# Block-causal attention and a rational FFN in float32 on one core: the causal mask moved from a matmul of its own into the unused half of the score passes' operands

## The chip, the cores and the metric

The kernel runs on one core of a Trainium2 chip. The core has a matrix engine (TensorE, PE in the profile, with its weight loads as PEld), a vector engine (VectorE, DVE), a scalar engine for activations and copies (ScalarE, ACT), GpSimd (POOL) and SyncE (SP), which here does nothing but issue transfers to the core's 16 DMA engines. Engines work on SBUF, 128 partitions wide; PE writes its sums into eight banks of PSUM. Each engine runs its instructions in the order that was fixed when the kernel was built, and waits on semaphores.

The metric is the device time of one execution in microseconds.

## The reference

Attention over 8 batches, 8 heads, 576 positions and 64 channels, with a causal mask by blocks of 64 positions, and then an FFN over the 4608 tokens whose activation is a quotient of polynomials; all in float32:

```python
scores = (1.0 / np.sqrt(D)) * np.matmul(q, k.transpose(0, 1, 3, 2))
mask = (pos[:, None] // 64) >= (pos[None, :] // 64)
scores = np.where(mask, scores, -1000000000.0)
scores = scores - np.max(scores, axis=-1, keepdims=True)
attn = np.exp(scores)
attn = attn / (np.sum(attn, axis=-1, keepdims=True) + 1e-09)
x = np.matmul(attn, v)            # then [B*S, H*D] = [4608, 512]

h = x @ w_in                      # [4608, 2048]
P = a[0] + a[1] * h + a[2] * h**2 + a[3] * h**3
Q = 1.0 + abs(b[0]) * abs(h) + abs(b[1]) * h**2
out = (P / (Q + 1e-06)) @ w_out   # [4608, 512]
```

## The kernel before

**Numbers in two parts.** Float32 precision is kept by splitting every operand into a high part h and a low part l that the matrix engine takes in one pass each.

**A pair of heads at a time.** The 32 pairs of heads (8 batches, 4 pairs each) are worked on one after the other. `load` brings q, k and v of a pair. `prep(p, 0)` transposes q of both heads on PE (L355) and writes its high part with ACT (L359) and its low part with DVE (L360) into a tile `hl`; `prep(p, 1)` does the same with k. `hl` has four slots of 576 columns, q high, k high, k low, q low, and one buffer: rows 0 to 63 belong to head 0, rows 64 to 127 to head 1. As soon as k is there too, three transfers for each head (L369 to L371) make a tile `kq` of it, over 128 rows: in the head's own rows q high, k high, k low, and in the other 64 rows q low, k high, k low. There are three buffers of `kq` (KQB), two of them for each pair.

**Scores.** `scores(p, t, j)` works on head j and query tile t (64, 128, 128, 128 and 128 queries against 64, 192, 320, 448 and 576 keys; the fifth in two pieces of 288). The first pass (L421) multiplies [q high; q low] by [k high; k high], the second (L422) by [k low; k low], so that both passes use all 128 rows. For t > 0 a third matmul in bf16 (L425) adds -2^30 where the first 64 queries of the tile meet the last 64 keys: `mrow` has it in row 0 of its first 64 columns, `mcol` has a one there. The row's maximum is taken by DVE (L426). `expo`, one step later, does the exponential on ACT (L438) and the division on DVE and POOL (L444 to L451). `transp` transposes the probabilities on PE (L470), and splits them (L475, L476) into `pt0`, `pt1` and `pt2`; `pv` multiplies them by v, for tiles 0 to 2 together and for tiles 3 and 4 together (L489), splits the result into a tile `xs` (L492, L493), and stores it to a scratch tensor `xscr` in DRAM (L494). Scores, transposes, products with v and the transposes of `prep` share five PSUM banks (`ps_a`); for the first four pairs some of them use the FFN's banks too.

**FFN.** It runs in units of 256 tokens by 256 hidden columns: `first` (24 matmuls, L201), an activation over ACT, POOL and DVE (L208 to L226), a split (L233, L234) and `second` (12 matmuls, L250). The hidden columns are done in two phases, 10 of the 16 blocks of 128 in phase 0, 6 in phase 1. Phase 0 runs between the steps of attention as soon as whole batches are done; phase 1 begins when attention has given its memory back. Weights are split into parts by the kernel itself, early on.

**Order.** `attn_steps` goes through 320 steps (pair, tile, head), ten to a pair. In a pair's steps the next pair is loaded at step 0 and prepared at steps 3 (q) and 5 (k); `transp` follows its scores by nine steps, `pv` by ten. The FFN gets its half-units spread over the steps (UP, UN, HOLD): from step 93 to step 333, 134 of them. This order of the program is a priority, not the order of execution: at build time a scheduler with a model of the engines' times goes through the instructions, issues what can run by then, hands out the buffers of a tag as they come free, and so fixes the queue of each engine.

Of the kernel before, what the change touches and what calls it, by code (L numbers as in the profile page):

```python
# [9 lines left out]
F32 = mybir.dt.float32  # L10
F32R = mybir.dt.float32r
I32 = mybir.dt.int32
U32 = mybir.dt.uint32
BF16 = mybir.dt.bfloat16
AF = mybir.ActivationFunctionType
ALU = mybir.AluOpType
AX = mybir.AxisListType
# [3 lines left out]
B, H, S, D = 8, 8, 576, 64  # L21
# [6 lines left out]
LEND = 4  # L28
RL = 3
C0 = 0  # L30
KQB = 3
XB = 3
HOLD = 6
ALAG3 = 10
# [9 lines left out]
LAG = (1, 2, 3)  # L44
GBUFS = 2
CBUFS = 2
NFA = 10
NFB = NF - NFA
NU = (NFA // 2, NFB // 2)
LP = 96  # L50
NL = S // LP
QSCALE = 0.125
NEG = -float(2 ** 30)
# [6 lines left out]
def attn_ffn_kernel(  # L60
# [11 lines left out]
    nc = tc.nc  # L72
    nc.scalar.preload_act_table_set("natural_log_exp_and_others")

    cpool = ctx.enter_context(tc.tile_pool(name="const", bufs=1))
    dpool = ctx.enter_context(tc.tile_pool(name="scratch", bufs=1, space=DRAM))
    ffn = ctx.enter_context(tc.tile_pool(name="ffn", bufs=2))
# [8 lines left out]

    ident = cpool.tile([128, 128], F32, name="ident")
    make_identity(nc, ident)
    mrow = cpool.tile([128, 128], BF16, name="mrow")
    mcol = cpool.tile([128, 64], BF16, name="mcol")  # L90
    nc.vector.memset(mrow, 0.0)
    nc.vector.memset(mrow[0:1, 0:64], NEG)
    nc.vector.memset(mcol, 0.0)
    nc.vector.memset(mcol[0:1, :], 1.0)
    coef = cpool.tile([128, 6], F32, name="coef")
    nc.gpsimd.dma_start(out=coef[:, 0:4], in_=ca.partition_broadcast(128))
    nc.gpsimd.dma_start(out=coef[:, 4:6], in_=cb.partition_broadcast(128))
# [198 lines left out]
    NK = [64, 192, 320, 448, 576]  # L296

    wpool = ctx.enter_context(tc.tile_pool(name="wA", bufs=1))
    with ExitStack() as actx:
        att = actx.enter_context(tc.tile_pool(name="att", bufs=2))  # L300
        apers = actx.enter_context(tc.tile_pool(name="apers", bufs=1))
# [2 lines left out]
        pt0 = [apers.tile([128, 1, 320], F32R, name=f"pt0{x}") for x in "hl"]  # L304
        pt1 = [apers.tile([128, 4, 256], F32R, name=f"pt1{x}") for x in "hl"]
        pt2 = [apers.tile([128, 9, 256], F32R, name=f"pt2{x}") for x in "hl"]

        vpad = [apers.tile([128, 128 + 4 * 192], F32R, name=f"vp{x}") for x in "hl"]
        for x in pt1:
# [2 lines left out]
            nc.vector.memset(x[:, 7:9, 0:128].bitcast(F32), 0.0)  # L312
        for x in vpad:
            nc.vector.memset(x.bitcast(F32), 0.0)


        NP = B * NPAIR
# [26 lines left out]
        def prep(p, which):  # L344

            s = st_[p]
            if which == 0:
                s["hl"] = att.tile([128, 4, S], F32R, name=f"hl{p}", tag="hl", bufs=1)
            raw, sc = (s["qr"], s["kr"])[which], (QSCALE, 1.0)[which]
            hl = s["hl"]  # L350
            h, l = (hl[:, 0], hl[:, 3]) if which == 0 else (hl[:, 1], hl[:, 2])
            for half in range(2):
                ps = bank(p - 1, f"tp{p}_{which}_{half}")[:, :3 * LP].rearrange("p (c t) -> p c t", c=3)
                for c in range(3):
                    nc.tensor.transpose(ps[:, c, :], raw[:, half * 3 + c].rearrange("p j d -> p (j d)"),  # L355
                                        ident[:LP, :LP])
                cs = slice(half * 288, half * 288 + 288)
                pf = ps.rearrange("p c t -> p (c t)")
                nc.scalar.activation(out=h[:, cs], in_=pf, func=AF.Copy, scale=sc)  # L359
                nc.vector.scalar_tensor_tensor(out=l[:, cs], in0=pf, scalar=sc, in1=h[:, cs].bitcast(F32),  # L360
                                               op0=ALU.mult, op1=ALU.subtract)
            if which == 1:


                for j in range(2):
                    kq = att.tile([128, 3, S], F32R, name=f"kq{p}_{j}", tag="kq", bufs=KQB)
                    src = hl[64 * j:64 * j + 64].bitcast(F32)
                    other = kq[64 - 64 * j:128 - 64 * j].bitcast(F32)
                    nc.sync.dma_start(out=kq[64 * j:64 * j + 64].bitcast(F32), in_=src[:, 0:3])  # L369
                    nc.sync.dma_start(out=other[:, 1:3], in_=src[:, 1:3])  # L370
                    nc.sync.dma_start(out=other[:, 0], in_=src[:, 3])  # L371
                    s["kq", j] = kq

        def vprep(p):
            vr = st_[p]["vr"]
# [24 lines left out]
        def pieces(t):  # L400
            return [(0, NK[t])] if t < 4 else [(0, 288), (288, 288)]

        def scores(p, t, j):
            s = st_[p]
            nq = NQ[t]
            if j == 0:
                pt = att.tile([128, 2, NK[t]], F32, name=f"p{p}_{t}", tag=f"p{t}", bufs=1)

                pk = att.tile([128, 2, 64], F32, name=f"pk{p}_{t}", tag="pk", bufs=2) if t > 0 else pt
                nm = att.tile([128, 2, 2], F32, name=f"nm{p}_{t}", tag="nm", bufs=4)  # L410
                sm = att.tile([128, 2, 2], F32, name=f"sm{p}_{t}", tag="sm", bufs=4)
                s[t] = (pt, pk, nm, sm)
            pt, pk, nm, sm = s[t]
            kq = s["kq", j]
            qs = slice(Q0[t], Q0[t] + 128)
            banks = []
            for i, (c0, w) in enumerate(pieces(t)):
                ww = max(w, 256)
                ps = ps_a.tile([128, 512], F32, name=f"s{p}_{t}_{j}_{i}", tag="a")
                last = t > 0 and c0 + w == NK[t]  # L420
                nc.tensor.matmul(ps[:, :ww], lhsT=kq[:, 0, qs], rhs=kq[:, 1, c0:c0 + ww], start=True, stop=False)  # L421
                nc.tensor.matmul(ps[:, :ww], lhsT=kq[:, 0, qs], rhs=kq[:, 2, c0:c0 + ww],  # L422
                                 start=False, stop=not last)
                if last:
                    nc.tensor.matmul(ps[:, w - 64:w], lhsT=mrow, rhs=mcol, start=False, stop=True)  # L425
                nc.vector.reduce_max(out=nm[:nq, j, i:i + 1], in_=ps[:nq, :w], axis=AX.X, negate=True)  # L426
                banks.append(ps)
            if t == 4:
                nc.vector.tensor_tensor(out=nm[:, j, 0:1], in0=nm[:, j, 0:1], in1=nm[:, j, 1:2], op=ALU.min)
            s[t, j] = banks  # L430
# [24 lines left out]
        def transp(p, t):  # L455
            pt, pk, _, _ = st_[p].pop(t)
            nq = NQ[t]
            nb = 1 + 2 * t
            groups = {1: [1], 3: [1, 2], 5: [1, 4], 7: [4, 3], 9: [3, 3, 3]}[nb]
            blk = 0  # L460
            for gi, gn in enumerate(groups):
                ps = bank(p, f"t{p}_{t}_{gi}").rearrange("p (c t) -> p c t", c=4)
                for i in range(gn):
                    x = blk + i
                    if x == 0:
                        src = pk[:nq].rearrange("q j k -> q (j k)")
                    else:
                        key = 64 + 128 * ((x - 1) // 2)
                        src = pt[:nq, (x - 1) % 2, key:key + 128]
                    nc.tensor.transpose(ps[:, i, :nq], src, ident[:nq, :nq])  # L470
                (hi, lo), b0, c0 = ((pt2, blk, Q0[t] - 320) if t > 2 else (pt0, 0, Q0[t]) if blk == 0 else
                                    (pt1, blk - 1, Q0[t] - 64))
                dh = hi[:, b0:b0 + gn, c0:c0 + nq]
                dl = lo[:, b0:b0 + gn, c0:c0 + nq]
                nc.scalar.copy(out=dh, in_=ps[:, :gn, :nq])  # L475
                nc.vector.tensor_tensor(out=dl, in0=ps[:, :gn, :nq], in1=dh.bitcast(F32), op=ALU.subtract)  # L476
                blk += gn

        def pv(p, g):
            b, hp = divmod(visits[p][0], NPAIR)  # L480
            vh, vl = vpad
            nb, w = ((5, 320), (9, 256))[g]
            o = ps_a.tile([128, 512], F32, name=f"o{p}_{g}", tag="a")
            for x in range(nb):
                s0 = 64 if (g == 0 and x > 0) else 0
                hi, lo = ((y[:, x] for y in pt2) if g else (y[:, 0] for y in pt0) if x == 0 else
                          (y[:, x - 1] for y in pt1))
                for i, (vv, pp) in enumerate(((vh, lo), (vh, hi), (vl, hi))):
                    nc.tensor.matmul(o[:, s0:w], lhsT=vblock(vv, x), rhs=pp,  # L489
                                     start=(x == 0 and i == 0), stop=(x == nb - 1 and i == 2))  # L490
            xs = att.tile([128, 2, 320], F32R, name=f"x{p}_{g}", tag="xs", bufs=1)
            nc.scalar.copy(out=xs[:, 0, :w], in_=o[:, :w])  # L492
            nc.vector.tensor_tensor(out=xs[:, 1, :w], in0=o[:, :w], in1=xs[:, 0, :w].bitcast(F32), op=ALU.subtract)  # L493
            nc.sync.dma_start(out=xscr[b][:, hp, :, g * 320:g * 320 + w], in_=xs[:, :, :w].bitcast(F32))  # L494
# [40 lines left out]

        wts, wsteps = split_weights(wpool, 0, NFA, F32R)
        load(0)
# [82 lines left out]
```

## Time and profile before

| | us |
|---|---|
| median of 3 runs | 1390.15 (1389.13 to 1396.89) |
| the profiled execution | 1389.48 |
| its span, first to last instruction | 1387.7 |
| PE busy | 1294.4 (93%) |
| DVE busy | 1029.0 (74%) |
| POOL busy | 955.3 (69%) |
| ACT busy | 909.7 (66%) |
| score passes, first to last start | 17.1 to 961.1 |
| DMA packets in 40 slices, total | 200.93 MB, mean 145 GB/s |

Busy times are unions of instructions' durations. Matmuls are pipelined: the duration of one is longer than the distance to the next, so what a matmul costs is read from start to start. A row of the timeline gives the start, the time from the first start to the last end, engine, line, operation, tiles, shape, how many in a row, and in brackets how long the engine was idle before and what ended it. A row that ends in `xN` and begins with `SPq` is the issue of a transfer; when it has landed is told by the list of DMA issues, as a median from issue to landing.

### The profile page before, as it was taken

Reading aid. Unit: us, or ns where it says so; the run is one execution under the profiler, and the core shown is the slowest. Engines: PE = TensorE matmul, PEld = TensorE weight load, DVE = VectorE, ACT = ScalarE, POOL = GpSimd, SP = SyncE. Lnnn points to the kernel's source line nnn. Section 1 sums busy time; section 2 is a strip of 40 time slices with the busy share of each in tenths; the row PEclk is TensorE's granted clock in tenths of the full one; section 3 lists DMA queues with packets and bytes.
Section 4 is the critical chain, followed back from the end, with each engine's and each line's share of the span. In section 5 each row is a group of like instructions: output and inputs, shape, how many; then the busy total and the mean of one; then the engine's idle time right before and its main releaser. Section 6 shows DMA issues by size and latency. Waiting matters only on the chain.

```text
span 1387.7 us, 25820 instructions
## 1 busy us (share of the span) xinstructions
PE 1294.4 (93%) x8736; PEld 1165.6 (84%) x8736; DVE 1029.0 (74%) x2048; ACT 909.7 (66%) x2250; POOL 955.3 (69%) x1240
## 2 busy tenths in 40 slices
PE   4677899999899989999999999999989999999998
PEld 3567788989788878888989999999979998999897
DVE  5898877788778867887767777766756676776665
ACT  4676777777677766776767777776545555555553
POOL 4888877687777757777767676766556655565564
PEclk9787899999999999999999999999999999999999
DMA  9778566666656665675654565651711333333332
GB/s 214 199 196 234 146 148 161 158 165 184 149 142 154 162 167 141 156 178 136 164 133 113 150 151 123 152 139 46 259 59 60 107 122 122 122 122 122 122 122 91
DMA packets 225635, 200.93 MB, mean 145 GB/s; under 512 B 132064, under 2 KB 195552, under 8 KB 225504
## 3 DMA queue, kind: packets, MB, share of 16 engines
q1 hardware_dynamic: 225440, 199.28, 54.2%
q8 instruction: 70, 1.15, 0.3%
q14 instruction: 61, 0.50, 0.1%
q0 software_dynamic: 64, 0.00, 0.0%
HBM read 98.57 MB, written 44.04 MB: 103 GB/s over the span
## 4 chain that ended last, share of the span: by engine, by line
PE 72%; DVE 9%; DMA 6%; POOL 5%; ACT 4%; issue 2%; SPq 1%; DVEq 0%; POOLq 0%; ACTq 0%
PE h L201 26%; PE o L250 25%; PE o L489 9%; PE t L470 4%; PE s L421 3%; PE s L422 3%; PE tp L355 2%; DMA x<-xscr 2%; DMA kq<-hl 2%; DVE nm L426 1%; ACT p L438 1%; POOL gl L234 1%; DVE v L225 1%; DVE u L224 1%; DMA xscr<-x 1%
## 5 line engine op out<-in xcount | busy, mean ns | idle before, releaser
L201 PE MATMUL h<-x,wih 128*128 128x256 f32 x2304 | 446.3, 289 | 12.0 <-DMA x<-xscr 7.9
L201 PEld LDWEIGHTS h<-x,wih 128*128 128x128 f32 x2304 | 372.3, 194 | 21.6 <-issue 7.6
L201 PE MATMUL h<-x,wil 128*128 128x256 f32 x1152 | 331.0, 287 | 0.0
L250 PE MATMUL o<-woh,gl 128*128 128x512 f32 x576 | 232.2, 403 | 7.9 <-POOL gl L234 6.8
L210 POOL TENSOR_SCALAR v<-u,bab 128x512 f32<-128x512 f32 x144 | 120.2, 835 | 165.0 <-ACT u L208 162.6
L250 PE MATMUL o<-woh,gh 128*128 128x512 f32 x576 | 227.9, 396 | 0.0
L250 PE MATMUL o<-wol,gh 128*128 128x512 f32 x576 | 227.0, 394 | 0.0
L426 DVE TENSOR_REDUCE nm<-s 128x1 f32<-128x288 f32 (+4 forms) x384 | 161.4, 427 | 84.8 <-PE s L425 49.9
L201 PEld LDWEIGHTS h<-x,wil 128*128 128x128 f32 x1152 | 223.2, 194 | 0.4
L234 POOL TENSOR_TENSOR gl<-s,gh 128x512 fp32r<-128x512 f32 x144 | 188.4, 1309 | 50.2 <-ACT gh L233 47.2
L438 ACT ACTIVATE p<-s,nm 128x288 f32<-128x288 f32 (+4 forms) x384 | 184.6, 484 | 47.1 <-DVE nm L426 34.8
L211 POOL TENSOR_TENSOR u<-v,u 128x512 f32<-128x512 f32 x144 | 190.2, 1321 | 9.8
L451 POOL TENSOR_SCALAR p<-p,rc 128x128 f32<-128x128 f32 (+3 forms) x256 | 165.0, 656 | 31.6 <-DVE rc L446 29.3
L208 ACT ACTIVATE u<-h 128x512 f32<-128x512 f32 x144 | 86.0, 597 | 123.5 <-PE h L201 116.9
L218 ACT ACTIVATE v<-u,qcb 128x512 f32<-128x512 f32 x144 | 104.6, 726 | 92.0 <-POOL u L211 91.4
L421 PE MATMUL s<-kq 128*128 128x256 f32 (+3 forms) x384 | 136.3, 357 | 24.0 <-DMA kq<-hl 11.2
L212 DVE TENSOR_TENSOR s<-s,h 128x512 f32<-128x512 f32 x144 | 98.6, 685 | 69.8 <-ACT s L209 68.9
L250 PEld LDWEIGHTS o<-woh,gl 128*128 128x128 f32 x576 | 109.4, 190 | 28.3 <-POOL gl L234 9.0
L250 PEld LDWEIGHTS o<-wol,gh 128*128 128x128 f32 x576 | 108.7, 189 | 22.4
L250 PEld LDWEIGHTS o<-woh,gh 128*128 128x128 f32 x576 | 109.3, 190 | 16.0
L470 PE MATMUL t<-ident,p 128*128 128x128 f32 (+1 forms) x672 | 113.0, 279 | 7.2 <-POOL p L451 2.3
L422 PE MATMUL s<-kq 128*128 128x256 f32 (+3 forms) x384 | 119.0, 312 | 0.0
(105 smaller groups left out, 2993.6 us busy)
## 6 DMA issues: line engine op xcount, KB each, us to landing
kq<-hl SPq DMA_DIRECT2D x64, 432.0 KB, 4.2
x<-xscr SPq DMA_DIRECT2D x96, 256.0 KB, 3.6
kq<-hl SPq DMA_DIRECT2D x64, 288.0 KB, 5.4
xscr<-x SPq DMA_DIRECT2D x32, 320.0 KB, 4.7
qr<-in_q_dram SPq DMA_DIRECT2D x64, 144.0 KB, 2.8
kr<-in_k_dram SPq DMA_DIRECT2D x64, 144.0 KB, 2.7
kq<-hl SPq DMA_DIRECT2D x64, 144.0 KB, 4.9
pscr<-os SPq DMA_DIRECT2D x18, 512.0 KB, 3.3
```

The source lines that it names most:

```text
L201: nc.tensor.matmul(h[:, j, :], lhsT=w[:, dc, fs], rhs=xs[dc // 2][:, dc % 2, hl, :], start=(dc == 0 and i == 0), stop=(dc == 3 and i == 2))
L210: nc.gpsimd.tensor_scalar(out=vt, in0=ut, scalar1=b1, scalar2=b0, op0=ALU.mult, op1=ALU.add)
L211: nc.gpsimd.tensor_tensor(out=ut, in0=vt, in1=ut, op=ALU.mult)
L234: nc.gpsimd.tensor_tensor(out=gl.rearrange("p j t -> p (j t)"), in0=st, in1=gh.rearrange("p j t -> p (j t)").bitcast(F32), op=ALU.subtract)
L250: nc.tensor.matmul(self.o[m], lhsT=g[:, j, ms], rhs=w[:, f, :], start=(u == 0 and j == 0 and i == 0), stop=(u == nu - 1 and j == 1 and i = ...
L421: nc.tensor.matmul(ps[:, :ww], lhsT=kq[:, 0, qs], rhs=kq[:, 1, c0:c0 + ww], start=True, stop=False)
L422: nc.tensor.matmul(ps[:, :ww], lhsT=kq[:, 0, qs], rhs=kq[:, 2, c0:c0 + ww], start=False, stop=not last)
L426: nc.vector.reduce_max(out=nm[:nq, j, i:i + 1], in_=ps[:nq, :w], axis=AX.X, negate=True)
L438: nc.scalar.activation(out=pt[:nq, j, c0:c0 + w], in_=banks[i][:nq, :w], func=AF.Exp, bias=nm[:nq, j, 0:1], scale=1.0, accum_out=sm[:nq, j ...
L451: nc.gpsimd.tensor_scalar(out=pt[:nq, jj, 64:n], in0=pt[:nq, jj, 64:n], scalar1=rc[:nq, jj:jj + 1], scalar2=1.0, op0=ALU.mult, op1=ALU.mult)
L470: nc.tensor.transpose(ps[:, i, :nq], src, ident[:nq, :nq])
L489: nc.tensor.matmul(o[:, s0:w], lhsT=vblock(vv, x), rhs=pp, start=(x == 0 and i == 0), stop=(x == nb - 1 and i == 2))
```

## The change

The mask moves into the first score pass, and the fourth product, low by low, goes. `kq` now has four slots: in the head's own rows q high, q high, k high, k low, and in the other 64 rows a mask over the queries, q low, a mask over the keys, k high. The first pass multiplies slot 0 by slot 2, that is q high by k high plus the mask; the second multiplies slot 1 by slot 3, that is q high by k low plus q low by k high. The mask over the keys has a one in row r where the key lies in block r, the mask over the queries has -2^30 in row r where the query lies in a block before r; so it masks all of the causal triangle. Both are built once on POOL, stored to DRAM (`mscr`), and copied into the other half of every `kq`.

For room, `hl` is halved: it holds q alone, then k alone, with one buffer, and `xs` shares that buffer (tag "hl"). So `prep` now makes its copies in two lots, four transfers for each head when q is there, two when k is.

The probabilities of tile 0 get a persistent tile `p0` whose rows 64 to 127 are zero, and are transposed over 128 rows.

```diff
-    mrow = cpool.tile([128, 128], BF16, name="mrow")
-    mcol = cpool.tile([128, 64], BF16, name="mcol")
-    nc.vector.memset(mrow, 0.0)
-    nc.vector.memset(mrow[0:1, 0:64], NEG)
-    nc.vector.memset(mcol, 0.0)
-    nc.vector.memset(mcol[0:1, :], 1.0)
...
+        p0 = apers.tile([128, 2, 64], F32, name="p0")
+        nc.vector.memset(p0[64:128], 0.0)
...
+        mscr = dpool.tile([64, 2, S], F32, name="mscr")
+        mask = ffn.tile([64, 2, S], F32, name="mask", tag="os")
+        nc.gpsimd.memset(mask[:, 1], 1.0)
+        nc.gpsimd.affine_select(out=mask[:, 1], in_=mask[:, 1], compare_op=ALU.is_ge, fill=0.0,
+                                base=0, pattern=[[1, S]], channel_multiplier=-64)
+        nc.gpsimd.affine_select(out=mask[:, 1], in_=mask[:, 1], compare_op=ALU.is_ge, fill=0.0,
+                                base=63, pattern=[[-1, S]], channel_multiplier=64)
+        nc.gpsimd.memset(mask[:, 0], NEG)
+        nc.gpsimd.affine_select(out=mask[:, 0], in_=mask[:, 0], compare_op=ALU.is_ge, fill=0.0,
+                                base=-1, pattern=[[-1, S]], channel_multiplier=64)
+        nc.sync.dma_start(out=mscr, in_=mask)
...
         def prep(p, which):
-            if which == 0:
-                s["hl"] = att.tile([128, 4, S], F32R, name=f"hl{p}", tag="hl", bufs=1)
-            hl = s["hl"]
-            h, l = (hl[:, 0], hl[:, 3]) if which == 0 else (hl[:, 1], hl[:, 2])
+            hl = att.tile([128, 2, S], F32R, name=f"hl{p}_{which}", tag="hl", bufs=1)
+            h, l = hl[:, 0], hl[:, 1]
...
-            if which == 1:
-                for j in range(2):
-                    kq = att.tile([128, 3, S], F32R, name=f"kq{p}_{j}", tag="kq", bufs=KQB)
-                    src = hl[64 * j:64 * j + 64].bitcast(F32)
-                    other = kq[64 - 64 * j:128 - 64 * j].bitcast(F32)
-                    nc.sync.dma_start(out=kq[64 * j:64 * j + 64].bitcast(F32), in_=src[:, 0:3])
-                    nc.sync.dma_start(out=other[:, 1:3], in_=src[:, 1:3])
-                    nc.sync.dma_start(out=other[:, 0], in_=src[:, 3])
-                    s["kq", j] = kq
+            for j in range(2):
+                if which == 0:
+                    s["kq", j] = att.tile([128, 4, S], F32R, name=f"kq{p}_{j}", tag="kq", bufs=KQB)
+                kq = s["kq", j]
+                src = hl[64 * j:64 * j + 64].bitcast(F32)
+                own = kq[64 * j:64 * j + 64].bitcast(F32)
+                other = kq[64 - 64 * j:128 - 64 * j].bitcast(F32)
+                if which == 0:
+                    nc.sync.dma_start(out=other[:, 0:3:2], in_=mscr)
+                    nc.sync.dma_start(out=own[:, 0], in_=src[:, 0])
+                    nc.sync.dma_start(out=own[:, 1], in_=src[:, 0])
+                    nc.sync.dma_start(out=other[:, 1], in_=src[:, 1])
+                else:
+                    nc.sync.dma_start(out=own[:, 2:4], in_=src)
+                    nc.sync.dma_start(out=other[:, 3], in_=src[:, 0])
...
         def scores(p, t, j):
-                pt = att.tile([128, 2, NK[t]], F32, name=f"p{p}_{t}", tag=f"p{t}", bufs=1)
+                pt = att.tile([128, 2, NK[t]], F32, name=f"p{p}_{t}", tag=f"p{t}", bufs=1) if t > 0 else p0
...
-                last = t > 0 and c0 + w == NK[t]
-                nc.tensor.matmul(ps[:, :ww], lhsT=kq[:, 0, qs], rhs=kq[:, 1, c0:c0 + ww], start=True, stop=False)
-                nc.tensor.matmul(ps[:, :ww], lhsT=kq[:, 0, qs], rhs=kq[:, 2, c0:c0 + ww],
-                                 start=False, stop=not last)
-                if last:
-                    nc.tensor.matmul(ps[:, w - 64:w], lhsT=mrow, rhs=mcol, start=False, stop=True)
+                nc.tensor.matmul(ps[:, :ww], lhsT=kq[:, 0, qs], rhs=kq[:, 2, c0:c0 + ww], start=True, stop=False)
+                nc.tensor.matmul(ps[:, :ww], lhsT=kq[:, 1, qs], rhs=kq[:, 3, c0:c0 + ww], start=False, stop=True)
...
         def transp(p, t):
+            np_ = 128 if t == 0 else nq
-                        src = pk[:nq].rearrange("q j k -> q (j k)")
+                        src = pk[:np_].rearrange("q j k -> q (j k)")
-                    nc.tensor.transpose(ps[:, i, :nq], src, ident[:nq, :nq])
+                    nc.tensor.transpose(ps[:, i, :np_], src, ident[:np_, :np_])
...
         def pv(p, g):
-            xs = att.tile([128, 2, 320], F32R, name=f"x{p}_{g}", tag="xs", bufs=1)
+            xs = att.tile([128, 2, S], F32R, name=f"x{p}_{g}", tag="hl", bufs=1)
```

KQB keeps its value of 3, and the steps at which `load` and `prep` stand in the order stay as they were.

More of the change, by code (lines that the diff above doesn't have):

```diff
@@ L13 @@
 U32 = mybir.dt.uint32
-BF16 = mybir.dt.bfloat16
 AF = mybir.ActivationFunctionType
@@ L30 @@
 C0 = 0
-KQB = 3
 XB = 3
@@ L46 @@
 CBUFS = 2
+KQB = 3
 NFA = 10
```

## Prediction

> **What bounds the kernel now.** I read the page first, then busy time by stage, then the timeline of TensorE (PE), the issuing queue (SP) and ScalarE (ACT) around one head pair, then the DMA issues.
>
> ```profile
> span 1387.7 us, 25820 instructions
> PE 72%; DVE 9%; DMA 6%; POOL 5%; ACT 4%; issue 2%; SPq 1%; DVEq 0%; POOLq 0%; ACTq 0%
> ...
> 17.00:139.00 122.00, 86.74 (x503) 73.16 (x503) 102.84 (x243) 83.50 (x252) 100.81 (x136) 0.82 0.84 213
> 139.00:961.00 822.00, 788.54 (x5586) 713.21 (x5585) 632.45 (x1379) 590.00 (x1605) 598.91 (x870) 0.99 0.59 148
> 961.00:1388.00 427.00, 414.81 (x2632) 375.99 (x2630) 286.85 (x407) 230.57 (x383) 249.77 (x222) 0.99 0.37 117
> ...
> L421 PE MATMUL s<-kq x384: 274/363/722, 17.1 to 961.1; 128*128 128x256 f32 x64, 128*128 128x288 f32 x64, 128*128 128x320 f32 x32, 128*128 128x448 f32 x32
> L201 PE MATMUL h<-x,wih x2304: 274/283/582, 133.9 to 1371.0; 128*128 128x256 f32 x192
> ```
>
> The first number of a stage row is its length, then come the busy times of PE, PE's weight loads, DVE, ACT and POOL, the granted clock, the DMA share and GB/s. The last two rows say from when to when score passes (L421) and FFN matmuls (L201) run. Three stages: 17 to 139 us, five pairs of heads almost without FFN (PE busy 71%, DVE 84%); 139 to 961 us, 27 pairs with FFN matmuls between them (PE busy 96%); and after 961 us FFN alone, which the change doesn't touch. So in the middle PE's queue sets the pace, and a matmul taken away there is worth its pitch, provided that attention still delivers on time. Whether it does is read from one pair, the one that starts at 511.22 us:
>
> ```profile
> 506.41 0.44 PE L422 MATMUL s<-kq 128*128 128x288 f32 x1
> ...
> 511.22 0.38 PE L421 MATMUL s<-kq 128*128 128x256 f32 x1
> 511.44 0.28 PE L422 MATMUL s<-kq 128*128 128x256 f32 x1
> 511.56 0.40 PE L201 MATMUL h<-x,wih 128*128 128x256 f32 x2
> 511.80 0.28 PE L201 MATMUL h<-x,wil 128*128 128x256 f32 x1
> ...
> 514.43 0.28 PE L421 MATMUL s<-kq 128*128 128x256 f32 x1
> ...
> 536.00 0.29 PE L422 MATMUL s<-kq 128*128 128x288 f32 x1
> ...
> 543.84 0.38 PE L421 MATMUL s<-kq 128*128 128x256 f32 x1
> ```
> ```profile
> 506.88 0.47 SPq L369 DMA_DIRECT2D kq<-hl  x1
> 507.40 0.59 SPq L370 DMA_DIRECT2D kq<-hl  x1
> 508.04 1.63 SPq L371 DMA_DIRECT2D kq<-hl  x1
> ...
> 518.82 0.49 SPq L371 DMA_DIRECT2D kq<-hl  x1
> ```
>
> The pass at 506.41 is the last one of head 0 of the pair before, and it ends at 506.85. The three issues at 506.88 to 508.04 stand right behind it: they fill kq of head 1 of the next pair, and of the three kq buffers the only one to come free is the one that this pass was reading. The next such pass ends at 536.00 + 0.29 = 536.29. So a pair is a stretch of scores S = 536.29 - 511.22 = 25.1 us, and a gap to the next pair's first pass of 543.84 - 536.29 = 7.6 us (4.4 us the time before, 506.85 to 511.22). In the gap nothing of the next pair's head 0 waits for a copy: its q and k halves lie in one four-slot hl and were copied earlier. Only head 1 is late.
>
> **The change, part by part.**
>
> Removed: 256 mask passes, eight to a pair.
>
> ```profile
> 520.78 0.31 PE L422 MATMUL s<-kq 128*128 128x320 f32 x1
> 520.93 0.20 PE L425 MATMUL s<-mcol,mrow 128*128 128x64 bf16 x1
> 520.97 0.36 PE L201 MATMUL h<-x,wih 128*128 128x256 f32 x1
> 521.17 0.28 PE L201 MATMUL h<-x,wil 128*128 128x256 f32 x1
> ...
> L425 PE MATMUL s<-mcol,mrow 128*128 128x64 bf16 x256 | 53.1, 208 | 0.0
> ```
>
> The mask pass takes PE at 520.93. Without it the FFN matmul starts there and its successor one pitch later; that pitch is 0.12 us (511.56 to 511.80 holds two), so at 521.05 and not 521.17. A mask pass is worth 0.12 us (bounds: 0.04, the distance to the next start, and its own 0.208), eight of them 1.0 us a pair, 27 x 1.0 = 26 us in the middle stage if PE binds. The Trainium skill ("TensorE: Matmul & The Clock Gate", section "Back-to-back issue gap") puts a matmul of 1 to 64 columns at a floor of about 25 ns; by it the masks would be worth an estimated 256 x 0.025 = 6 us. The trace disagrees: 64 columns don't cover the next weight load, and the successor comes 0.12 us later.
>
> Score passes: two before, two after, of the same shapes and with a weight load each as now. Nothing.
>
> Transposes of tile 0 over 128 rows:
>
> ```profile
> 543.64 0.27 PE L470 MATMUL t<-ident,p 64*128 64x64 f32 x1
> ```
>
> From it to the next pass at 543.84 are 0.20 us, against 0.12 behind a full-height pass: 32 x 0.08, at most 3 us gained. The other end is 32 x 0.03 lost for the 64 columns more. I take 0.
>
> Moved: the copies into kq, and the buffer they come from. This decides.
>
> ```profile
> kq<-hl SPq DMA_DIRECT2D x64, 432.0 KB, 4.2
> ...
> kq<-hl SPq DMA_DIRECT2D x64, 288.0 KB, 5.4
> ...
> xscr<-x SPq DMA_DIRECT2D x32, 320.0 KB, 4.7
> ...
> kq<-hl SPq DMA_DIRECT2D x64, 144.0 KB, 4.9
> ...
> 517.01 0.40 ACT L359 ACTIVATE hl<-tp 128x288 fp32r<-128x288 f32 x1
> ...
> 518.35 0.44 DVE L360 SCALAR_TENSOR_TENSOR hl<-tp,hl 128x288 fp32r<-128x288 f32 x1
> ```
>
> Now six copies a pair, then twelve: for each head the mask (2 slots, 288 KB), q high twice and q low (144 KB each), then k (288 KB) and k high (144 KB). That is 2 x (1152 - 864) = 576 KB more a pair. At a DMA share of 0.59 I take the volume as hidden; six issues more cost SP six times about 0.5 us, counted only where they stand in the chain.
>
> The chain: hl holds q alone, then k alone, in one buffer, which the outputs of pv (xs) now share. So k can't be written before all copies of q have landed, and those of head 1 can't be issued before the last pass of head 0 of the running pair has let go of its kq buffer. From the end of that pass:
> - four issues instead of three: the last goes out after 0.2 + 0.47 + 0.59 + 0.5 = 1.8 us and lands 4.9 us later: 6.7 us;
> - k written into hl, two halves on ACT and DVE: 517.01 to 518.79, 1.8 us;
> - k to head 0's kq, two issues, landed: 0.2 + 0.5 + 4.9 = 5.6 us.
>
> So the first pass of the next pair can't start before 6.7 + 1.8 + 5.6 = 14.1 us after the last head-0 pass, where today it is 4.4 to 7.6. On its engine the write of k is an ACT instruction: behind it queue the exps and the FFN's activations, and DVE and POOL wait for those.
>
> What this costs depends on how far S shrinks while FFN matmuls move into the gap. Ends: S stays 25.1 (period 39.2), or falls to what attention needs alone. For that, a pair before the FFN:
>
> ```profile
> 88.15 0.39 PE L421 MATMUL s<-kq 128*128 128x256 f32 x1 [0.78 <-ACT p L438]
> ...
> 100.26 0.29 PE L422 MATMUL s<-kq 128*128 128x288 f32 x1
> ...
> 109.29 0.28 PE L421 MATMUL s<-kq 128*128 128x256 f32 x1
> ...
> 139.41 0.39 PE L421 MATMUL s<-kq 128*128 128x256 f32 x1
> ```
>
> S is 100.55 - 88.15 = 12.4 us here, which gives a period of 26.5. Neither end is likely: part of the FFN stays beside the scores, and the transposes of k, ready early, hold two of the five score banks until hl is free. I take the middle, 18.8, less the 1.0 of the masks: 17.8, a period of 31.9. Today 27 periods fill 139.41 to 961, 30.4 each. So **+1.5 x 27 = +40 us**.
>
> The first five pairs have no FFN to fill a gap. Today's gap there is 109.29 - 100.55 = 8.7; 14.1 - 8.7 = 5.4, less the masks' 1.0, times five: **+22 us** (bounds 0, if the weight work on DVE sets the pace, and 27). The first pair waits for the mask's trip through DRAM and for q's eight copies ahead of k: between 0 and one such 5.4, I take **+3**.
>
> Sum, against the profiled execution's own time of 1389.5 us (span 1387.7 and 1.8 around it; the median of the three runs, 1390.15, is 0.05% above): 1389.5 + 40 + 22 + 3 = **1455 us**.
>
> **Rivals.**
>
> 1. *PE stays the bound, and the change is faster.* The FFN fills the longer gap.
>
> ```profile
> 539.29 0.49 PE L250 MATMUL o<-woh,gl 128*128 128x512 f32 x1 [0.42 <-POOL gl L234]
> ...
> 542.17 0.28 PE L489 MATMUL o<-pt2l,vph 128*128 128x256 f32 x1
> ```
>
> One FFN unit is 514.43 - 511.56 = 2.9 us of first and 542.17 - 539.29 = 2.9 us of second matmuls; the pacing lays 134 half-units over 240 score steps, 2.8 units in ten steps, 16 us a pair: more than 14.1. S would have to go to 15 us; from a period below 29.4 it decides. Then 26 + 2 us go, half of the early 25 stays: 1389.5 - 28 + 12 = 1374 us (1360 to 1382). Against it: one bank for the FFN's first product, and orders fixed ahead, so that a copy late by a microsecond stops ACT and with it all.
>
> 2. *The masks go, the steady gap is hidden, the early one isn't:* 1389.5 - 28 + 25 = 1386 us, within 0.5%.
>
> 3. *xs stands in front of k in the shared buffer.*
>
> ```profile
> L492 ACT CAST x<-o 128x320 fp32r<-128x320 f32 x32 | 13.6, 426 | 11.0 <-PE o L489 8.2 <-PE s L425 1.3 <-issue 1.2
> L493 DVE TENSOR_TENSOR x<-o,x 128x320 fp32r<-128x320 f32 x32 | 15.4, 481 | 3.2 <-ACT x L492 3.2
> ```
>
> If pv's first group is ready while q holds the buffer, its output goes first: 0.43 + 0.48 + 0.4 + 4.7 = 6.0 us in the chain. On every pair 1455 + 27 x 6.0 = 1617 us, on every other 1536. It decides as soon as pv comes before the fifth tile's scores.
>
> 4. *The mask pass was free,* hidden as a short pass, so the change does less than it says: no 1.0 a pair, 1389.5 + 27 x 2.5 + 27 + 3 = 1487 us. By the skill's 25 ns the estimate would be 1480.
>
> **How the numbers follow.** Forecast (the chain binds with S near 18; its own range 1400 to 1510) 0.46; rival 3 0.14; rival 4 0.06; rival 1 0.24; rival 2 0.10. A measurement of this kernel tells about 0.5% from no change, so slower 0.66, same 0.10, faster 0.24. The range leaves out the lower third of rival 1 and the upper half of rival 3: 1365 to 1540 us.
>
> **What would show it.** In the profile after: the distance from the last head-0 pass of a pair to the next pair's first pass, 14 us or more (at 8 the chain is wrong); idle time of ACT's hl write put down to the copies kq<-hl, and of xs to xscr; the last score pass later than 1000 us against 961 now, and PE's busy share in the middle stage down from 96% to about 90%; the FFN stage behind it 427 us long as now. L425 gone and the FFN matmul's successor 0.12 us earlier shows the mask's price. If the last score pass comes before 945 us, the FFN filled the gap and rival 1 holds. The prediction is wrong at its root if q's buffer is let go before the running pair's head 0 is done.

## The result and the profile after

The changed kernel takes 1791.1 us (1787.2 to 1801.1, 4 runs) against 1392.1 us for the kernel before: the ratio is 1.287, with a 95% interval of 1.280 to 1.294. The forecast was slower, 1455 us with a range up to 1540: the sign and the place were right, the size wasn't. The loss is 399 us and not 63.

The page of the changed kernel, its busy times by stage (length, then PE, PE's weight loads, DVE, ACT, POOL, granted clock, DMA share, GB/s), and the row of its first score pass (L432, before L421):

```profile
span 1799.1 us, 25698 instructions
PE 43%; DMA 18%; DVE 14%; ACT 8%; POOL 6%; SPq 6%; issue 4%; ACTq 0%; DVEq 0%; POOLq 0%
...
25.00:184.00 159.00, 96.20 (x466) 81.66 (x466) 104.74 (x247) 86.72 (x254) 102.03 (x143) 0.74 0.67 178
184.00:1383.00 1199.00, 941.21 (x5454) 824.14 (x5453) 653.50 (x1387) 614.05 (x1618) 583.17 (x871) 0.85 0.43 115
1383.00:1799.00 416.00, 402.35 (x2542) 363.55 (x2540) 282.95 (x397) 221.75 (x367) 241.31 (x215) 0.99 0.36 117
...
L432 PE MATMUL s<-kq x384: 276/391/742, 24.9 to 1382.2; 128*128 128x256 f32 x64, 128*128 128x288 f32 x64, 128*128 128x320 f32 x32, 128*128 128x448 f32 x32
```

The three stages end at pair five and at the last score pass, as before. First five pairs: 159 us instead of 122. Then 27 pairs: 1199 us instead of 822, with PE busy for 78% and not 96%. The FFN behind them: 416 us, 11 less than before. PE's share of the chain that ended last falls from 72% to 43%, and DMA's rises from 6% to 18%. So nearly all of the loss lies in the attention stage, as 14 us on each of its 27 pairs.

One gap shows what they are. These rows are the changed kernel's timelines of PE, SP and ACT from the last head-0 pass of one pair to the first pass of the next (start, length, engine, line; in brackets how long the engine was idle before, and what ended that):

```profile
575.59 0.30 PE L433 MATMUL s<-kq 128*128 128x288 f32 x1
...
595.16 0.28 PE L432 MATMUL s<-kq 128*128 128x256 f32 x1
```
```profile
575.92 0.56 SPq L378 DMA_DIRECT2D kq<-mscr  x1
576.52 0.60 SPq L379 DMA_DIRECT2D kq<-hl  x1
577.16 0.60 SPq L380 DMA_DIRECT2D kq<-hl  x1
577.80 0.60 SPq L381 DMA_DIRECT2D kq<-hl  x1
...
582.85 0.36 SPq L503 DMA_DIRECT2D xscr<-x  x1
...
588.84 0.48 SPq L383 DMA_DIRECT2D kq<-hl  x1
```
```profile
581.87 0.42 ACT L501 CAST x<-o 128x320 fp32r<-128x320 f32 x1 [0.77 <-DMA kq<-hl]
...
585.34 0.71 ACT L365 ACTIVATE hl<-tp 128x288 fp32r<-128x288 f32 x2 [1.14 <-DMA xscr<-x]
...
595.99 0.37 ACT L501 CAST x<-o 128x256 fp32r<-128x256 f32 x1 [4.31 <-DMA kq<-hl]
```

The pass ends at 575.89. Right behind it go the four copies for head 1, one of the mask and three of q. They have landed when ACT starts on xs at 581.87: 6.0 us. But xs takes the buffer first, and k only gets it when xs is in DRAM, at 585.34: another 3.5 us. k is written, its copies are issued from 588.84 on, and the next pair begins at 595.16. The gap is 19.3 us, where the one in the prediction's rows was 7.6. Not all of its end is the chain: by the trace head 0's two copies of k have landed at 592.89, and the pass stands 2.3 us longer behind FFN matmuls in PE's queue. The last row is the second cost: an ACT instruction that waits 4.31 us for a copy, with exps and the FFN's activations behind it in ACT's queue.

Over the whole run, the waits of ACT for these buffers (us in total, times, longest):

```profile
ACT x L501 <- DMA kq<-hl: 103.8, 45, 6.3
...
ACT hl L365 <- DMA xscr<-x: 44.8, 31, 4.1
```

The kernel before has one such row, of hl; xs waited for no copy:

```profile
ACT hl L359 <- DMA kq<-hl: 3.9, 2, 3.6
```

What follows uses two numbers worked out from such timelines: S, from a pair's first pass to the end of its last head-0 pass, and the gap from there to the next pair, both as means over the 25 pairs from the seventh to the thirty-first. Before: S 24.7, gap 6.0. After: S 27.9, gap 17.3. The links of that gap, as means over the same pairs: 6.0 us until q's copies have landed, 3.8 until k's write starts, with one xs between them in each of the 25, and 7.6 from there to the next pair's first pass.

### The profile page after: what moved, and what is told of

Read it like the earlier page. It is cut to its first block, busy times and chain, and to the rows that moved or that the text cites. A ratio compares the mean times of both kernels' runs of the same rounds, so it can differ in the third digit from the quotient of the medians.

```text
span 1799.1 us, 25698 instructions
## 1 busy us (share of the span) xinstructions
PE 1444.2 (80%) x8480; PEld 1272.7 (71%) x8480; DVE 1048.2 (58%) x2045; ACT 928.1 (52%) x2250; POOL 934.7 (52%) x1245
## 4 chain that ended last, share of the span: by engine, by line
PE 43%; DMA 18%; DVE 14%; ACT 8%; POOL 6%; SPq 6%; issue 4%; ACTq 0%; DVEq 0%; POOLq 0%
PE h L194 17%; PE o L243 13%; DMA kq<-hl 10%; PE o L498 3%; PE t L479 3%; DMA xscr<-x 3%; PE s L432 3%; PE s L433 2%; DMA x<-xscr 2%; POOL gl L227 2%; DVE nm L434 2%; ACT p L446 2%; DMA kr<-in_k_dram 2%; PE tp L361 1%; DVE u L217 1%
## 5 line engine op out<-in xcount | busy, mean ns | idle before, releaser
L194 PE MATMUL h<-x,wih 128*128 128x256 f32 x2304 | 471.5, 302 | 47.4 <-DVE s L206 20.6
L194 PEld LDWEIGHTS h<-x,wih 128*128 128x128 f32 x2304 | 397.1, 207 | 66.1 <-issue 28.0
L432 PE MATMUL s<-kq 128*128 128x256 f32 (+3 forms) x384 | 155.9, 410 | 116.2 <-DMA kq<-hl 37.1
L194 PEld LDWEIGHTS h<-x,wil 128*128 128x128 f32 x1152 | 238.5, 207 | 0.2
L479 PE MATMUL t<-ident,p 128*128 128x128 f32 x672 | 133.8, 314 | 79.7 <-DVE hl L366 37.9
L432 PEld LDWEIGHTS s<-kq 128*128 128x128 f32 x384 | 85.5, 224 | 150.6 <-issue 53.0
L459 POOL TENSOR_SCALAR p<-p,rc 128x128 f32<-128x128 f32 (+3 forms) x256 | 149.9, 597 | 38.6 <-DVE rc L454 38.1
L479 PEld LDWEIGHTS t<-ident,p 128*128 128x128 f32 x672 | 92.8, 160 | 101.0 <-ACT p L446 41.8
L395 POOL TENSOR_TENSOR vpl<-vr,vph 128x256 fp32r<-128x256 f32 (+1 forms) x128 | 75.1, 594 | 155.5 <-ACT vph L394 113.0
L455 POOL TENSOR_TENSOR pk<-p,rc 128x128 f32<-128x128 f32 x128 | 57.3, 448 | 184.4 <-PE t L479 179.3
```

Source lines behind the costliest of these rows:

```text
L194: nc.tensor.matmul(h[:, j, :], lhsT=w[:, dc, fs], rhs=xs[dc // 2][:, dc % 2, hl, :], start=(dc == 0 and i == 0), stop=(dc == 3 and i == 2))
L459: nc.gpsimd.tensor_scalar(out=pt[:nq, jj, 64:n], in0=pt[:nq, jj, 64:n], scalar1=rc[:nq, jj:jj + 1], scalar2=1.0, op0=ALU.mult, op1=ALU.mult)
L479: nc.tensor.transpose(ps[:, i, :np_], src, ident[:np_, :np_])
```

## The experiments

Each ratio is to runs of the kernel before that were made beside it, whose medians lie between 1390.7 and 1393.1 us.

| kernel | us | ratio to before, 95% interval | S | gap |
|---|---|---|---|---|
| before | 1392 | 1 | 24.7 | 6.0 |
| after | 1791.1 | 1.287 (1.280 to 1.294) | 27.9 | 17.3 |
| e2_half: before, hl halved | 1587.5 | 1.141 (1.136 to 1.146) | 27.6 | 10.2 |
| e3_share: before, xs in hl's buffer | 1472.9 | 1.059 (1.054 to 1.064) | 25.1 | 8.5 |
| e4_half_share: both | 1789.6 | 1.286 (1.282 to 1.291) | 31.1 | 13.8 |
| e5_xs_os: after, xs elsewhere | 1639.3 | 1.177 (1.172 to 1.183) | 25.7 | 13.1 |
| e10_half_kqb4: before, halved, four kq | 1450.6 | 1.042 (1.038 to 1.046) | 26.3 | 6.3 |
| e7_hl2: after, two hl buffers, room made | 1506.3 | 1.082 (1.079 to 1.085) | 25.2 | 7.2 |
| e8_room_xs: before, same room made | 1516.7 | 1.089 (1.085 to 1.092) | 25.4 | 7.4 |
| e13_klate: after, k's transposes late | 1692.1 | 1.216 (1.211 to 1.220) | 20.1 | 20.7 |
| e12_ps3: before, three score banks | 1610.7 | 1.157 (1.153 to 1.161) | 29.6 | 8.8 |
| e1_nomask: before without mask pass | 1397.3 | 1.003 (1.001 to 1.006) | 24.6 | 6.3 |
| e11_mask3: before, mask pass three times | 1404.1 | 1.009 (1.006 to 1.012) | 25.0 | 5.9 |
| e6_p0: before, 128-row transposes | 1390.5 | 0.999 (0.997 to 1.000) | 24.5 | 5.9 |
| e14_up30: before, other FFN pacing | 1377.8 | 0.990 (0.988 to 0.992) | 24.1 | 6.4 |
| e15_up30_nomask: that, without mask pass | 1397.6 | 1.005 (1.003 to 1.006) | 24.5 | 6.2 |

**The buffer, without the mask.** The first question was whether the memory plan alone does it (theory A) or the mask's copies (theory B). So the plan was put into the kernel before, one half at a time, with the mask pass and the three-slot kq kept.

```diff
 # e2_half: q and k each take the one buffer of hl, copies in two lots
+            hl = att.tile([128, 2, S], F32R, name=f"hl{p}_{which}", tag="hl", bufs=1)
...
+            for j in range(2):
...
+                if which == 0:
+                    nc.sync.dma_start(out=own[:, 0], in_=src[:, 0])
+                    nc.sync.dma_start(out=other[:, 0], in_=src[:, 1])
+                else:
+                    nc.sync.dma_start(out=own[:, 1:3], in_=src)
+                    nc.sync.dma_start(out=other[:, 1:3], in_=src)
 # e3_share: hl keeps its four slots
-            xs = att.tile([128, 2, 320], F32R, name=f"x{p}_{g}", tag="xs", bufs=1)
+            xs = att.tile([128, 4, S], F32R, name=f"x{p}_{g}", tag="hl", bufs=1)
...
 # e4_half_share: both
```

> The kernel before with its mask pass and three-slot kq, but hl halved: q alone, then k alone, in one buffer, copied in two lots (eight copies for a pair, the same 1728 KB); xs keeps its own buffer. Theory A (the one buffer is a chain: k can't be written before q's copies for head 1 have landed, and these wait for the running pair's head 0): the gap from the last head-0 pass to the next pair's first pass goes from 6 to about 13 us, the stretch of scores stays near 25, so 38 a pair and about 1600 us in all. Theory B (the added 576 KB and six issues a pair are what costs): no change beyond two issues a pair, 1392 to 1400 us.

> The kernel before with one thing changed: xs takes its buffer from hl's tag (four slots, one buffer). Theory A: the gap stays near 6 to 8 us, since k is written with q, but the outputs of pv wait on ACT for the copies of hl to land and the next q waits for xscr: 20 to 150 us more, 1410 to 1540. Theory B: 1392.

> Both of these buffer edits on the kernel before, mask pass kept, no mask copies: the memory plan of the changed kernel without its mask. Theory A: as slow as the changed kernel, 1740 to 1830 us, with a gap of about 17 us. Theory B: below 1420.

All three times came out as theory A has it; the split of e2_half (gap 10.2 and S 27.6, expected about 13 and 25) and of e4_half_share (gap 13.8, expected about 17) didn't: more of the loss lies in S. Their rows of the first score pass (first and last start) and of ACT's and PE's waits:

```profile
L421 PE MATMUL s<-kq x384: 278/366/744, 18.5 to 1177.8; 128*128 128x256 f32 x64, 128*128 128x288 f32 x64, 128*128 128x320 f32 x32, 128*128 128x448 f32 x32
...
PE s L421 <- DMA kq<-hl: 86.6, 29, 4.9
```
```profile
L421 PE MATMUL s<-kq x384: 274/368/741, 18.5 to 1047.0; 128*128 128x256 f32 x64, 128*128 128x288 f32 x64, 128*128 128x320 f32 x32, 128*128 128x448 f32 x32
...
ACT x L492 <- DMA kq<-hl: 49.5, 26, 3.8
```
```profile
L421 PE MATMUL s<-kq x384: 277/386/722, 18.4 to 1374.8; 128*128 128x256 f32 x64, 128*128 128x288 f32 x64, 128*128 128x320 f32 x32, 128*128 128x448 f32 x32
```

The first fence is e2_half, where the scores wait 29 times for a copy (4 times and 11.2 us before), the second e3_share, where ACT stands still for xs, the third both. Halving hl costs 195 us, sharing it 80, and the two together 397, which is 122 more than the sum. In the table the excess is 4.2 us a pair, 1.1 of them in the gap and 3.1 in S, which is taken up below. With both, the kernel before is as slow as the changed one: 1789.6 and 1791.1. The mask's move, its 576 KB of copies a pair and the 128-row transposes then come to next to nothing, taken together.

**Taking the plan back from the changed kernel.**

```diff
 # e5_xs_os, and in e7_hl2 as well; in e10_half_kqb4 and e8_room_xs the same,
 # from the tag "xs" of the kernel before
-            xs = att.tile([128, 2, S], F32R, name=f"x{p}_{g}", tag="hl", bufs=1)
+            xs = ffn.tile([128, 2, 320], F32R, name=f"x{p}_{g}", tag="os")
 # e10_half_kqb4: e2_half with that, and
-KQB = 3
+KQB = 4
 # e7_hl2: after with that, and
-            hl = att.tile([128, 2, S], F32R, name=f"hl{p}_{which}", tag="hl", bufs=1)
+            hl = att.tile([128, 2, S], F32R, name=f"hl{p}_{which}", tag="hl", bufs=2)
 # and for room
-XB = 3
+XB = 2
-                pk = att.tile([128, 2, 64], F32, name=f"pk{p}_{t}", tag="pk", bufs=2) if t > 0 else pt
+                pk = att.tile([128, 2, 64], F32, name=f"pk{p}_{t}", tag="pk", bufs=1) if t > 0 else pt
 # e8_room_xs: before with XB 2, one pk, xs in "os"
```

> The changed kernel with one edit: xs takes a tile of the FFN's tag os (two buffers) instead of hl's buffer. Theory A (two costs, the chain q - k in one buffer, and xs between them): the second one goes, so about what the halved hl alone cost, 1570 to 1620 us, gap 10 to 13 us. Rival (copies of the mask and twelve issues carry a good part): stays above 1680.

> The kernel before with halved hl in one buffer (as in e2_half), xs in the tag os, and four kq buffers instead of three, so that q's copies for head 1 no longer wait for the running pair's head 0. If that wait makes the chain: gap back to 6 to 8 us and 1395 to 1440 us. If it is the serial use of one buffer by q and k, whatever it waits for: above 1500.

> The changed kernel with two buffers for the halved hl, xs in the tag os, and room made for it (XB 2 for 3, one buffer for pk). Mask in the free half and twelve copies a pair stay. Theory A: nothing is left of the loss; within 1% of the kernel before with the same room made (e8_room_xs), gap near 6 to 8 us. Rival (traffic, issues): over 3% above it.

> Control for e7_hl2: the kernel before with XB 2, one buffer for pk, xs in the tag os. Little: 1390 to 1430 us.

e5_xs_os wins 152 us back, 1639; that is 19 above the range given, and 52 above e2_half. Only 15 of the 52 are there by the last score pass (1192.6 against 1177.8 us), 6 of them since the first pair starts at 24.7 instead of 18.5. The other 37 come behind it, where 449 us of FFN are left instead of 412; e10_half_kqb4, which has xs among the FFN's staging tiles too and no copies of the mask, has 452 left. e10_half_kqb4 shows what the chain hangs on. With a fourth kq buffer q's copies for head 1 needn't wait for the running pair, and the gap is 6.3 us although q and k still go through one buffer; of e2_half's 195 us, 58 are left, 11 more than the upper end expected; 25 of these 58 lie in the FFN behind the scores (452 us, 427 before).

e7_hl2 and its control say what the change is worth without its buffers. Both are slow, since the room itself costs 125 us, far more than expected: the scores end at about 1000 us, and the FFN behind them takes 84 and 89 us longer than before. By e10_half_kqb4 some 25 of that go with xs in "os"; the two x tiles instead of three and the single pk weren't tried apart.

```profile
L432 PE MATMUL s<-kq x384: 274/365/722, 17.7 to 989.4; 128*128 128x256 f32 x64, 128*128 128x288 f32 x64, 128*128 128x320 f32 x32, 128*128 128x448 f32 x32
```
```profile
L421 PE MATMUL s<-kq x384: 274/365/741, 17.5 to 1000.6; 128*128 128x256 f32 x64, 128*128 128x288 f32 x64, 128*128 128x320 f32 x32, 128*128 128x448 f32 x32
```

The first is e7_hl2, the second the control. At equal room the mask in the free half, with twelve copies a pair, is 10 us faster (1506.3 against 1516.7, 0.7%). That is less than another order of the queues moves this kernel (1.0%, below), and e7_hl2 also has another plan for hl, so no gain of the mask is shown by it. But traffic and issues cost nothing that can be seen here either, and theory B falls twice.

**Why the scores didn't get faster.** In the changed kernel 5.8 us of FFN matmuls run in a gap and 1.7 before (matmuls counted in each gap, at 0.12 and 0.23 us). The FFN did move, and with 4.1 us of it gone S should have been below 21; it grew to 27.9. PE stands idle for 6.3 us of it, where it was 1.0 before, and its granted clock within S is 0.86, not 0.99. Two things can hold S: PSUM banks that wait for the buffer, or stalls elsewhere. These rows are PE's timeline in the pair that starts at 595.16, with ACT's rows beneath:

```profile
605.54 0.31 PE L498 MATMUL o<-pt0l,vph 128*128 128x320 f32 x1
...
607.42 0.66 PE L361 MATMUL tp<-ident,kr 96*128 96x96 f32 x6
...
626.58 0.29 PE L433 MATMUL s<-kq 128*128 128x288 f32 x1
```
```profile
634.45 0.42 ACT L501 CAST x<-o 128x320 fp32r<-128x320 f32 x1 [1.37 <-DMA kq<-hl]
...
637.78 0.71 ACT L365 ACTIVATE hl<-tp 128x288 fp32r<-128x288 f32 x2 [0.89 <-DMA xscr<-x]
```

pv's sums (L498) take a bank at 605.54 and give it up after 634.45; k's transposes (L361) take two at 607.42 and give them up after 637.78. So from 607 to the last head-0 pass at 626.87 the scores and the transposes of probabilities have two banks of five. As a mean over the same pairs k's two banks are held 27.6 us and the first pv's 24.7, where it is 2.7 and 4.9 in the kernel before.

```diff
 # e13_klate: after, with k prepared at step 9 and its transposes ordered
 # on PE behind the running pair's last head-0 pass
-OFFS = {5:(0,3,5)}
+OFFS = {5:(0,3,9)}
...
+                with tc.issue_after(st_[p - 1]["last"].ins) if which == 1 and p > 0 else ExitStack():
...
 # e12_ps3: before
-    ps_a = ctx.enter_context(tc.tile_pool(name="ps_a", bufs=5, space=PSUM))
+    ps_a = ctx.enter_context(tc.tile_pool(name="ps_a", bufs=3, space=PSUM))
```

> The changed kernel with k's transposes held back on PE until behind the running pair's last head-0 pass (k prepared at step 9, not 5, and an order given for PE). They end before q's copies have landed, so the chain is no longer than before; only the two score banks that wait with k's transposes, 27.6 us of every 45, are free meanwhile. If these banks keep the stretch of scores long: S from 27.9 to 23 or less, 1600 to 1700 us. If it is the stalls on ACT's queue or the lower granted clock: S stays at 27 to 28, 1760 to 1810 us.

> The kernel before with three score banks instead of five and nothing else. Read in the attention stage only, since the FFN of phase 1 uses these banks too. If three banks are too few for the scores: S from 24.7 to 28 or more and the last score pass later than 1050 us (961 now). If five were plenty: S within 1 us and the last pass before 990 us.

Both agree with the banks. With k's transposes late S falls from 27.9 to 20.1 us, and with three banks in the kernel before it rises from 24.7 to 29.6, the last score pass going from 961 to 1194 us:

```profile
L421 PE MATMUL s<-kq x384: 277/384/739, 17.7 to 1193.6; 128*128 128x256 f32 x64, 128*128 128x288 f32 x64, 128*128 128x320 f32 x32, 128*128 128x448 f32 x32
```

e12_ps3 shows that banks alone can do it, with hl and xs as before. e13_klate isn't as clean: ACT's waits for the buffer within S, 2.0 us a pair in the changed kernel, are gone too, and 19 fewer matmuls run within S. In e2_half ACT doesn't wait for the buffer within S, k's two banks are held 19.0 us, and S is 27.6. Banks aren't all of S, though: e10_half_kqb4 holds k's two for 3.1 us only and has S at 26.3, with the short gap of 6.3 us to put the FFN in.

e13_klate is only 99 us faster and not more, since its gap grew to 20.7. ACT's timeline in one of its gaps says why:

```profile
585.41 0.43 ACT L504 CAST x<-o 128x320 fp32r<-128x320 f32 x1 [1.23 <-DMA kq<-hl]
...
591.53 0.37 ACT L504 CAST x<-o 128x256 fp32r<-128x256 f32 x1 [1.02 <-DMA xscr<-x]
...
595.94 0.71 ACT L366 ACTIVATE hl<-tp 128x288 fp32r<-128x288 f32 x2 [2.65 <-DMA xscr<-x]
```

Now both outputs of pv stand in front of k. The bank experiment lengthened the very chain that it left in place.

**What the mask pass is worth.** e1_nomask and e15_up30_nomask leave out the mask pass, so that their scores are unmasked.

```diff
 # e1_nomask: before
-                    nc.tensor.matmul(ps[:, w - 64:w], lhsT=mrow, rhs=mcol, start=False, stop=True)
...
 # e11_mask3: before
+                    for x in range(3):
+                        nc.tensor.matmul(ps[:, w - 64:w], lhsT=mrow, rhs=mcol, start=False, stop=x == 2)
 # e14_up30: before; e15_up30_nomask: with e1_nomask's edit
-UP = 25
+UP = 30
```

> The kernel before without its mask pass (L425 left out, so the scores stay unmasked). If a mask pass costs PE 0.12 us, 27 pairs of eight in the stage where PE binds give 26 us: 1366 us against 1392. If it is hidden as a short pass (0.04 us each) 10 us or less: 1382 to 1392.

> The kernel before with each mask pass done three times (the entries are masked by three times the value). If a mask pass costs PE its 0.12 us wherever PE is busy: 2 x 216 x 0.12 = 52 us more, 1440 to 1450. If PE has room for it: 1393 to 1410.

> The kernel before with the FFN's pacing at its start changed (UP 30 for 25), which gives the queues another order. Nothing else: 1380 to 1400 us.

> The same without the mask pass (scores stay unmasked). If a mask pass costs 0.12 us and the first comparison lost it to an unlucky order: 15 to 26 us below e14_up30. If the time it frees is spent waiting: within 7 us of e14_up30.

Without the pass the kernel isn't faster: +0.3%, 1397.3 us, which is above both of the ranges expected. With three it is 0.9% slower, 12 us for 512 more passes, 0.023 us each. The middle stage of e1_nomask, and a triple pass of e11_mask3:

```profile
139.00:961.00 822.00, 770.09 (x5294) 704.46 (x5293) 625.13 (x1362) 580.65 (x1585) 599.75 (x860) 0.98 0.60 149
```
```profile
504.95 0.26 PE L426 MATMUL s<-mcol,mrow 128*128 128x64 bf16 x3
505.05 0.31 PE L471 MATMUL t<-ident,pk 128*128 128x128 f32 x1
```

PE is 18.5 us less busy in the same 822 us (770.1 against 788.5), but these end before the stage does, whose last score pass comes at 977 us, not at 961. Over the whole of it, 139 to 977 us, PE is busy for 786.1 us, nearly as long as before, and waits for 52 us instead of 33. What it waits for more wasn't found. The triple pass takes 0.10 us from its start to its successor's, so an added pass costs 0.03 us. The Trainium skill's floor of about 25 ns ("TensorE: Matmul & The Clock Gate", section "Back-to-back issue gap"), which the prediction had set aside for a pitch of 0.12, agrees with that and with the run's 0.023.

Another order of the queues moves the kernel as much as all of the mask: e14_up30 changes one number of the FFN's pacing and is 1.0% faster than before, 1377.8 us, while the same without the mask pass is 20 us slower than that, which neither of the two outcomes expected allowed for. So in neither of the two orders is there a gain of 26 us. Why the kernel without the pass is slower in the second stays open. e14_up30 is the fastest kernel of this study.

**128-row transposes alone.**

> The kernel before with tile 0's probabilities in a persistent tile with zero rows, transposed over 128 rows: 32 transposes. At most 3 us faster, at most 1 us slower; 1389 to 1395 us. More than 0.5% either way would be the order of the queues, not the transposes.

Inside the range: 1390.5 us, with an interval that holds no change. Its edit is the p0 part of the change, put into the kernel before.

## Why the prediction was wrong

Worked out for the two profiled executions, whose spans differ by 411 us:

- **The steady pairs.** Forecast +40 us, measured 1199 - 822 = +377. The step that failed is the middle value of S. The prediction had "the transposes of k, ready early, hold two of the five score banks until hl is free" and then took "the middle, 18.8, less the 1.0 of the masks: 17.8". S was 27.9, outside both ends (25.1 and 12.4). Those banks, and pv's as a third, were held most of a pair, and e12_ps3 shows that S grows by 4.9 us when two banks are missing; how much of S is banks and how much ACT's waits and the slower clock stays open. A pair took 45.2 us where 31.9 were forecast: 10.1 of the 13.3 are S, 3.2 the gap.
- **The gap.** Forecast 14.1 us as a lower bound, from 6.7 + 1.8 + 5.6. Measured in the mean 6.0 + 3.8 + 7.6 = 17.3 (rounded): q's copies as forecast, the write of k and its copies as forecast (1.8 + 5.6 = 7.4), and 3.8 of xs between them that the sum put at nothing. e10_half_kqb4 confirms what holds the first link. In the pair shown it was 6.0, 3.5 and 9.8; there 1.5 us pass after k's write before its first copy is issued, behind loads of v in SP's queue, and 2.3 behind FFN matmuls.
- **Rival 3** put xs in front of k, with a chance of 0.14 and 1617 us if on every pair. It came true on every one of the 25 pairs, at 3.8 us and not 6.0; in the pair shown the transfer to xscr landed in 2.4 us and not 4.7. Its price of 1617 us still falls 174 short, as it rests on the same S. The signs named came out crosswise: it is xs that waits for kq's copies (103.8 us), and hl that waits for xscr (44.8), as it has to be with xs in front of k. It should have been part of the forecast: the shared tag is in the diff, and pv comes in the same steps as the preparation of k.
- **The first five pairs.** Forecast +22, measured 159 - 122 = +37. Their gaps are 16.2 us in the mean, where 14.1 was the forecast, and the masks' 1.0 a pair didn't come: S fell by 0.3. **The first pair** starts at 24.9 instead of 17.1: +8, not +3. k's first write waits 10.8 us for q's copies, some of which are issued behind copies of the mask; e2_half, with no mask to copy, starts at 18.5.
- **The FFN behind attention** was to stay at 427 us; it is 416.
- **The mask pass.** Forecast as 1.0 us a pair within S, and 26 us if PE binds. Measured: nothing gained when it is left out. The pitch of 0.12 us was read rightly as a distance, but an added pass costs 0.03 us (e11_mask3). And PE's busy 96% in the middle stage was taken for a bound, while e1_nomask shows that the stage doesn't get shorter when the passes go. Rival 4 came true in this.
- **Hidden work.** The 576 KB more a pair and the six issues were costed at nothing; e4_half_share and e7_hl2 bear that out, but for the first pair. The 128-row transposes at 0: e6_p0 bears that out.

## What to carry to other kernels

A buffer with one slot is a queue: list who writes it, what each reader waits for before it lets go, and add the links up over one period, everyone who shares the slot included. Then ask what each waiting writer holds meanwhile (here three of five PSUM banks and ACT's queue), because what the forecast missed lay there for the larger part: the chain was 3 us a pair longer than forecast, and the stretch beside it 10. A plan that halves a buffer to make room for a gain of 2% is best tried alone, without the gain: e4_half_share takes the whole loss with none of the change.

## What the hardware showed

PE ran slower in the idle pattern of the changed kernel. The granted clock in the middle stage was 0.85 against 0.99 before, and PE was busy for 941 us, where it was 788.5 before with 216 mask passes more and some 84 other matmuls fewer. These rows, from PE's timeline of the changed kernel, show FFN matmuls behind a pause:

```profile
590.72 0.48 PE L194 MATMUL h<-x,wih 128*128 128x256 f32 x2 [2.21 <-DVE pt0l L485]
...
592.30 0.63 PE L194 MATMUL h<-x,wih 128*128 128x256 f32 x2
592.72 0.41 PE L194 MATMUL h<-x,wil 128*128 128x256 f32 x1
592.94 0.63 PE L194 MATMUL h<-x,wih 128*128 128x256 f32 x2
...
594.80 0.40 PE L194 MATMUL h<-x,wih 128*128 128x256 f32 x2
595.04 0.28 PE L194 MATMUL h<-x,wil 128*128 128x256 f32 x1
```

From 592.30 to 592.94 three matmuls take 0.64 us, 0.21 each; at 594.80 two take 0.24, the usual 0.12. The granted clock is 0.50 from 591.3 to 594.7. The Trainium skill ("TensorE: Matmul & The Clock Gate", section "Part 1: The HAM clock gate (the "warmup" mystery)") has PE's clock at half rate after an idle window of about 3.4 us until it has been busy for as long. The trace agrees in the two rates and in 3.4 us at the slow one. It differs in what brings the slow rate on: the pause here is 2.21 us. In the changed kernel's trace the clock falls to 0.50 56 times; PE had been idle for the whole of the 3.41 us before in one of these, and busy for a quarter to a half of them in 45. So here a stretch that was half idle was mostly enough, without a pause of 3.4 us; the measurement decides.

Idle time thus comes with a slower PE: e2_half, with less of it, had a mean clock of 0.921, the changed kernel 0.872, the kernel before 0.973. How much of the 153 us that PE was busier lay on the path that sets the end was not tried.
